# Linear attention and Fourier feed-forward on one core: the second sweep's preparation set on a grid of points, its first pair read from SBUF, weights run through in alternating direction

## The chip, the cores and the metric

The kernel runs on one core of one Trainium2 chip. The metric is the time of one execution in microseconds (us); lower is better. The kernel before was timed three times: 1113.9, 1119.21 and 1117.34 us, median 1117.34.

The engines are named as in the profile: PE (matrix multiplications; PEld is its loading of weights, which overlaps), DVE (vector engine), ACT (scalar engine), POOL (GpSimd), SP (which here issues nearly all DMAs). Each works through its own queue in order; semaphores tie the queues together.

## What is computed

The reference, cut to what matters (8 batches, 8 heads, 576 tokens, head size 64, so 4608 tokens of width 512; hidden width 2048):

```python
kv  = einsum('bhsd,bhse->bhde', k, v)
out = einsum('bhsd,bhde->bhse', q, kv)
x   = (out / rms(out) * g_norm), heads side by side     # [8, 576, 512]
u   = x + real(fft(fft(x, axis=1), axis=2))
un  = (u - mean(u)) / sqrt(var(u) + 1e-6)
result = u + max(un @ w_ch1, 0) @ w_ch2
```

## The kernel before

The 4608 tokens are 9 blocks of 512 (BT), each of 4 tiles of 128 (TPB). The hidden width is 16 slices of 128, called f. Each float32 product is made of three passes (high times high, high times low, low times high), so a 512-wide product over 512 channels is 12 matmuls.

**Stage 1** (until about 362 us in the profile) does attention, Fourier transform and the slices f = 0 to 2 of the feed-forward for every block. A planner (`Plan`) sets its order. It leaves in DRAM: `u_scr` (the tokens u), `part_scr` (the feed-forward part of f = 0 to 2), and `unT_scr` (the normalised tokens, transposed, high and low part; the scaling by 1/sqrt(var) is still missing, it is applied later as `scale`).

**First sweep** (37 steps, L1529 to L1554). One step is one block j and one slice f: `first` (12 matmuls and a relu, split by ACT and DVE into `hh` and `hl`) and then `second` of the step before it (12 matmuls into 4 accumulators). All 9 blocks run f = 3 to 5; block 0 (`LONE`) runs the remaining f = 6 to 15 as well, and thereby finishes. Beside it `sum_w` and `split_w` (one of 20 units in each of the first 20 steps) convert the weights of f = 6 to 15 from their 64-bit input and write them to `w1_scr` and `w2_scr`, in NG = 5 quarters g of two slices. The results of f = 3 to 5 of blocks 1 to 8 go to DRAM as `next_scr` (ACT copies into one of 3 `lp` buffers, L1513, then a DMA, L1514).

**Second sweep** (L1561 to the end). Blocks 1 to 8 form 4 pairs: (8, 7), (6, 5), (4, 3), (2, 1). A loop of 20 rounds (4 pairs times 5 quarters) does in each 7 products `mult` of 6 matmuls each and 8 tile outputs of 6 matmuls each, 90 matmuls in all. The 7 products are Strassen's scheme: two blocks and two slices are combined into sums, so 7 products stand for 8. Every round loads its quarter's weights, `w1c` (1792 KB, `load_w1c`) and `w2c` (1024 KB, `load_w2c`), into one of two buffers. Each pair must be prepared:

- `prep_u`: read 8 tiles of u (`us`), take their variance on DVE (`bn_stats`, L1476), make `scale` of it with ACT's square root and four tiny DVE operations, and write `scale` to DRAM. Tiles whose tokens stand in mirrored order are read by an indirect DMA that POOL issues (L1462).
- `prep_z`: read `unT_scr` back (z and `low`), add the two on POOL (L1608), read `scale` back spread over all partitions (`wide`), multiply on POOL (L1610).
- `prep_t`: three new differences and one in place on POOL (L1618 to L1621).
- `prep_b`: split each of the 7 operands into high (ACT, L1360) and low (DVE, L1361).
- `prep_acc`: read `part_scr` and `next_scr`, add them on POOL (L1637), scale on ACT (L1485), add to `us` on POOL (L1488).

The first pair's preparation stands in the program after the first sweep's end; that of pair p+1 is written behind the rounds of pair p, and the operands are split in the last of them (`turn_over`). Where each instruction lands in its engine's queue is left to the scheduler after 300 us of the plan (`PIN_UNTIL`); only `plan.pin` ties instructions to the order in which they are written.

Of the kernel before, what the change touches and what calls it, by code (L numbers as in the profile page):

```python
# [9 lines left out]
F32 = mybir.dt.float32  # L10
# [9 lines left out]
EPS = 1e-6  # L20
# [273 lines left out]
def kernel(  # L294
# [52 lines left out]
    left = ExitStack()  # L347
    base = left.enter_context(tc.tile_pool(name="base", bufs=1))
    wA = left.enter_context(tc.tile_pool(name="wA", bufs=1))
# [970 lines left out]
    wB1[0].tile([P, PAD_RIGHT // 4], F32, name="pad_right")  # L1320
# [4 lines left out]
    mid = left  # L1325
    work = mid.enter_context(tc.tile_pool(name="work", bufs=1, reuse_waits="tile"))
    extra = mid.enter_context(tc.tile_pool(name="extra", bufs=1, reuse_waits="tile"))
    wq = mid.enter_context(tc.tile_pool(name="wq", bufs=2, reuse_waits="tile"))
    lone_pool = mid.enter_context(tc.tile_pool(name="lone", bufs=1, reuse_waits="tile"))

    LONE = 0
    PAIRS = [(j, j - 1) for j in range(NBLK - 1, 0, -2)]
# [136 lines left out]
    def fetch_block(j, tile_):  # L1469
        mv = tiny.tile([P, TPB, 2], F32, name="bmv")  # L1470
        uts = []
        for i in range(TPB):
            ut = tile_()
            fetch_u(j, i, ut)
            st = tiny.tile([P, 6], F32, name="bst")
            nc.vector.bn_stats(st, ut)  # L1476
# [6 lines left out]
    def add_part(j, i, ut, part, scale):
        t = j * TPB + i
        nc.scalar.activation(  # L1485
            part, part, AF.Identity, scale=scale[:, i : i + 1], bias=p0c[:, t : t + 1]
        )
        nc.gpsimd.tensor_tensor(ut, ut, part, ALU.add)  # L1488

    def lone_in():  # L1490
        lone["u"], lone["scale"] = fetch_block(
            LONE, lambda: lone_pool.tile([P, DM], F32, name="lu", tag="lu", bufs=TPB)
        )
        for i in range(TPB):
            n = LONE * TPB + i
            part = lone_pool.tile([P, DM], F32, name="lp", tag="lp", bufs=3)
            nc.sync.dma_start(part, part_scr[n * P : (n + 1) * P])
            acc = lone["acc"][i]
            nc.gpsimd.tensor_tensor(acc, acc, part, ALU.add)
            add_part(LONE, i, lone["u"][i], acc, lone["scale"])  # L1500

    def second(seg, hpair, f):
        j, fs = seg
        for i in range(TPB):
# [6 lines left out]
            if j != LONE:  # L1511
                part = lone_pool.tile([P, DM], F32, name="lp", tag="lp", bufs=3)
                nc.scalar.copy(part, acc_t[i])  # L1513
                nc.sync.dma_start(next_scr[t * P : (t + 1) * P], part)  # L1514
            elif fs is first_fs:
                part = lone_pool.tile([P, DM], F32, name="la", tag="la", bufs=TPB)
                nc.scalar.copy(part, acc_t[i])
                lone.setdefault("acc", []).append(part)
            elif f < NF - 1:
                part = lone["acc"][i]  # L1520
                nc.vector.tensor_tensor(part, acc_t[i], part, ALU.add)
            else:
                ut = lone["u"][i]
                nc.vector.scalar_tensor_tensor(
# [333 lines left out]
```

## Time and profile before

The profiled execution took 1116.74 us; its span from first to last instruction is 1114.9 us.

| engine | busy us | share of span | instructions |
|---|---|---|---|
| PE | 984.7 | 88% | 5950 |
| PEld | 819.4 | 73% | 5950 |
| DVE | 686.0 | 62% | 1198 |
| ACT | 392.7 | 35% | 747 |
| POOL | 500.1 | 45% | 434 |

The DMAs moved 235.71 MB, 211 GB/s on average; the largest shares are w1c (20 loads of 1792 KB) and w2c (20 loads of 1024 KB). The clock granted to PE was 0.949 of full speed on average. PE is the busiest engine, but its 88% is an average over stages that differ: the stretches in which it waits are what a change to the order of other work can reach.

### The profile page before, as it was taken

What the parts mean: (1) busy time and instruction counts of PE and PEld (TensorE: products, weight loads), DVE (VectorE), ACT (ScalarE), POOL (GpSimd) and SP (SyncE); (2) the same over time, 40 slices, a digit from 0 to 9 for tenths busy, and PEclk for the clock granted to TensorE, in tenths of its full rate; (3) what the DMA queues carried; (4) which work ended last, traced back from release to release, by engine and by line L of the source; (5) the groups of instructions that cost most, each with busy time, mean ns of one, the idle gap of its engine ahead of it and who ended that gap; (6) DMA issues with size and microseconds to landing.
All of it is one profiled execution on the core that took longest, in us unless ns stands there. A gap on an engine that the chain in (4) does not pass through costs nothing.

```text
span 1114.9 us, 16128 instructions
## 1 busy us (share of the span) xinstructions
PE 984.7 (88%) x5950; PEld 819.4 (73%) x5950; DVE 686.0 (62%) x1198; ACT 392.7 (35%) x747; POOL 500.1 (45%) x434
## 2 busy tenths in 40 slices
PE   5999999999999999899950259999869996999998
PEld 4888898888788887788840147777658875888887
DVE  4697877676986899942204236465546754575554
ACT  3557556565442443322310123151114311241110
POOL 2648767856531444430543567664257324700000
PEclk9999999999999999999985579999889998899999
DMA  9899858735568895663786258679756775445422
GB/s 224 224 221 246 265 150 229 216 129 198 194 215 293 302 361 193 259 249 126 255 269 269 48 131 276 190 245 347 190 131 253 290 236 173 174 185 179 155 91 76
DMA packets 130627, 235.71 MB, mean 211 GB/s; under 512 B 57982, under 2 KB 83122, under 8 KB 120052
## 3 DMA queue, kind: packets, MB, share of 16 engines
q1 hardware_dynamic: 126868, 227.07, 62.8%
q0 software_dynamic: 1920, 6.29, 2.2%
q10 hardware_dynamic: 1760, 1.31, 0.4%
q8 instruction: 47, 0.77, 0.3%
q14 instruction: 32, 0.26, 0.1%
HBM read 164.61 MB, written 70.03 MB: 210 GB/s over the span
## 4 chain that ended last, share of the span: by engine, by line
PE 62%; DMA 19%; DVE 7%; POOL 6%; issue 4%; ACT 1%; SPq 0%; POOLq 0%; DVEq 0%; ACTq 0%
PE acc L1685 12%; PE ps_h L1652 9%; DMA up<-next_scr 7%; PE acc L493 6%; PE ps_h L475 6%; PE ps_h L1441 6%; PE acc L1452 6%; PE ps_o L754 4%; PE ps_f L908 4%; DMA us<-u_scr,rowidx 2%; PE ps_k L659 2%; PE ps_f L968 2%; DMA next_scr<-lp 2%; POOL up L1637 2%; DMA z<-unT_scr 2%
## 5 line engine op out<-in xcount | busy, mean ns | idle before, releaser
L1685 PE MATMUL acc<-w2c,hh 128*128 128x512 f32 x640 | 202.7, 399 | 11.1 <-issue 11.1
L488 DVE SCALAR_TENSOR_TENSOR hl<-ps_h,hh 128x512 fp32r<-128x512 f32 x144 | 98.2, 686 | 135.7 <-ACT hh L485 135.0
L485 ACT ACTIVATE hh<-ps_h 128x512 fp32r<-128x512 f32 x144 | 84.9, 594 | 242.2 <-PE ps_h L1441 84.2
L1652 PE MATMUL ps_h<-b,w1c 128*128 128x512 f32 x360 | 97.6, 408 | 62.6 <-ACT b L1360 51.5
L1685 PEld LDWEIGHTS acc<-w2c,hh 128*128 128x128 f32 x640 | 123.7, 194 | 39.2 <-issue 12.6
L1652 PE MATMUL ps_h<-t,w1c 128*128 128x512 f32 x480 | 123.7, 408 | 32.3 <-ACT t L1360 18.9
L1652 PEld LDWEIGHTS ps_h<-t,w1c 128*128 128x128 f32 x480 | 94.1, 198 | 55.8 <-ACT t L1360 19.6
L1695 DVE TENSOR_TENSOR us<-acc,us 128x512 f32<-128x512 f32 (+1 forms) x161 | 106.4, 679 | 38.2 <-PE acc L1685 37.5
L1652 PEld LDWEIGHTS ps_h<-b,w1c 128*128 128x128 f32 x360 | 70.1, 197 | 80.5 <-ACT b L1360 52.0
L1685 PE MATMUL acc<-w2c,hl 128*128 128x512 f32 x320 | 126.6, 396 | 0.0
L1637 POOL TENSOR_TENSOR up<-up,up 128x512 f32<-128x512 f32 x32 | 46.8, 1463 | 62.3 <-DMA up<-next_scr 50.7
L1685 PEld LDWEIGHTS acc<-w2c,hl 128*128 128x128 f32 x320 | 61.6, 192 | 13.3
L1485 ACT ACTIVATE up<-up,p0c,rs_yb 128x512 f32<-128x512 f32 x32 | 25.9, 814 | 127.0 <-POOL up L1637 122.1
L794 POOL TENSOR_TENSOR x<-x,gb 96x512 f32<-96x512 f32 (+1 forms) x42 | 53.6, 1296 | 33.0 <-ACT x L771 21.8
L493 PE MATMUL acc<-w,hh 128*128 128x512 f32 x216 | 67.6, 399 | 0.0
L475 PE MATMUL ps_h<-unTh,w 128*128 128x512 f32 x216 | 67.6, 394 | 0.0
L1476 DVE BATCH_NORM_STATS2 bst<-us 128x6 f32<-128x512 f32 x32 | 21.1, 680 | 66.4 <-DMA us<-u_scr,rowidx 38.0
L1452 PE MATMUL acc<-w,hh 128*128 128x512 f32 x216 | 61.3, 390 | 0.0
L1441 PE MATMUL ps_h<-unTh,w 128*128 128x512 f32 x192 | 59.5, 391 | 1.4 <-DVE wa L1354 1.4
L1669 DVE TENSOR_TENSOR ps_h<-ps_h,s 128x512 f32<-128x512 f32 x60 | 40.1, 694 | 31.3 <-ACT s L1741 22.4
L1608 POOL TENSOR_TENSOR z<-z,low 128x1024 f32<-128x1024 f32 x16 | 39.9, 2493 | 39.0 <-DMA z<-unT_scr 28.5
L1610 POOL TENSOR_TENSOR z<-z,wide 128x1024 f32<-128x1024 f32 x16 | 38.7, 2437 | 38.0 <-DMA wide<-scale_scr 28.8
(178 smaller groups left out, 2072.5 us busy)
## 6 DMA issues: line engine op xcount, KB each, us to landing
w1c<-w_scr SPq DMA_DIRECT2D x20, 1792.0 KB
w2c<-w_scr SPq DMA_DIRECT2D x20, 1024.0 KB
raw<-in_moe_w_ch_dram SPq DMA_DIRECT2D x32, 512.0 KB
unT_scr<-unTh SPq DMA_DIRECT2D x9, 1024.0 KB
unT_scr<-unTl SPq DMA_DIRECT2D x9, 1024.0 KB
part_scr<-part SPq DMA_DIRECT2D x36, 256.0 KB
w_scr<-w1q SPq DMA_DIRECT2D x5, 1792.0 KB
km<-in_k_dram SPq DMA_DIRECT2D x32, 256.0 KB
```

What stands on the lines that cost most here:

```text
L475: nc.tensor.matmul(ps, w[c][:, kc * P : (kc + 1) * P], unT[a][:, kc, :], start=(idx == 0), stop=(idx == 3 * KC - 1),)
L485: nc.scalar.activation(hh, ps, AF.Relu)
L488: nc.vector.scalar_tensor_tensor(hl, ps, 0.0, hh.bitcast(F32), ALU.max, ALU.subtract)
L493: nc.tensor.matmul(acc, hpair[a][:, i * P : (i + 1) * P], w[c], start=(first and n == 0), stop=(last and n == 2),)
L754: nc.tensor.matmul(pss[s].t[:n, at : at + D], fqs[side].t[half, m, :n], kvt.t[half, m], start=True, stop=True,)
L794: nc.gpsimd.tensor_tensor(v_, v_, gb[:n].unsqueeze(1).to_broadcast([n, H, D]), ALU.mult)
L1441: nc.tensor.matmul(ps, w1_of(f, c, kc), unTs[j][a][:, kc, :], start=(idx == 0), stop=(idx == 3 * KC - 1),)
L1452: nc.tensor.matmul(acc, hpair[a][:, i * P : (i + 1) * P], w2_of(f, c), start=(first_ and n == 0), stop=(last_ and n == 2),)
L1637: nc.gpsimd.tensor_tensor(two_[0], two_[0], two_[1], ALU.add)
L1652: nc.tensor.matmul(ps, w[:, A_OF[m], c, kc * P : (kc + 1) * P], b[:, a, kc * BT : (kc + 1) * BT], start=(fresh and idx == 0), stop=(done a ...
L1685: nc.tensor.matmul(ps, hpair[a][:, i * P : (i + 1) * P], w2c[n][:, r, c], start=(idx == 0), stop=(idx == 5),)
L1695: nc.vector.tensor_tensor(ut[:, cols], ps[:, cols], ut[:, cols], ALU.add)
```

## The change

The arithmetic of the result stays; what moves is where and when the second sweep is prepared.

- Pairs are now (2, 1), (8, 7), (6, 5), (4, 3). Blocks 3, 2, 1 are the last of the first sweep, so the transposed tokens of blocks 2 and 1 still lie in SBUF (`unTs`). `z_from` adds them there, without reading `unT_scr` again. `second` adds the f = 3 to 5 result of these two blocks straight from PSUM to `us` (one DVE operation a tile) instead of passing it through `next_scr`.
- From step 28 (`closing`, block 3's first) the first pair's preparation stands in the first sweep, at a step number for each job. For this the buffers move: `base` goes to the right side of SBUF, and the left side is given to the second sweep at step 28.
- From step 28 on everything is pinned (`plan.pin`): each of the five queues keeps the order in which it is written.
- In the rounds, 15 points are counted (after each of the 7 products and 8 outputs, 6 matmuls apart); each job of the next pair's preparation has a point. z is read in halves of 256 KB into 3 `low` buffers. `part_scr` and `next_scr` tiles are no longer added to one another: each is scaled on ACT and added to `us` on POOL (`more_part`), 16 of each a pair instead of 8 ACT operations and 16 POOL ones.
- Odd pairs go through the quarters backwards. A quarter that is still in a buffer isn't loaded again: 14 loads of `w1c` and of `w2c` instead of 20.
- In the first sweep the 20 weight units are spread to one every 1.3 steps, with 5 `wa`, 3 `wp` and 4 `lp` buffers, and `split_w` follows `sum_w` by two steps.

```diff
-    left = ExitStack()
-    base = left.enter_context(tc.tile_pool(name="base", bufs=1))
+    low_ctx = ExitStack()
+    base = low_ctx.enter_context(tc.tile_pool(name="base", bufs=1, side="right"))
...
-    PAIRS = [(j, j - 1) for j in range(NBLK - 1, 0, -2)]
+    PAIRS = [(2, 1)] + [(j, j - 1) for j in range(NBLK - 1, 2, -2)]
...
+    unit_at = {round(n * 1.3): n for n in range(len(units))}
...
+    for j in (7, 8, LONE, None, 6, None, 5, None, 4, None, None, 3, 2, 1):
...
+            if j in PAIRS[0]:
+                nc.vector.scalar_tensor_tensor(
+                    us[j][i], acc_t[i], scale_of[j][:, i : i + 1], us[j][i], ALU.mult, ALU.add
+                )
...
+    def sides(step):
+        if step - LAG in unit_at:
+            split_w(*units[unit_at[step - LAG]])
+        if step in unit_at:
+            units_in(unit_at[step] + 3)
+            sum_w(*units[unit_at[step]])
+        for job in jobs.pop(step, ()):
+            job()
...
+    def low_slot():
+        return lop.tile([P, BT], F32, name="low", tag="low", bufs=3)
...
+    def w1_in(n):
+        g = quarter(n)
+        if w_held.get(("1", g)) == n - 1 or w_held.get(("1", g)) == n - 3:
+            w1c[n] = w1c[w_held["1", g]]
+        else:
+            t = w1c[n] = wcp[g % 2].tile([P, 7, 2, HK], F32R, name="w1c", tag="w1c")
+            nc.sync.dma_start(t.rearrange("p q c n -> p (q c n)").bitcast(F32), w1_scr[g])
+        w_held["1", g] = n
...
+    s0 = closing
+    for s_, j in enumerate(PAIRS[0]):
+        for i in range(TPB):
+            at(s0 + s_, u_in, j, i, lambda: us_slot(0))
+            at(s0 + 2 + s_, u_stats, j, i)
+            at(s0 + 3 + s_ + (i > 1), part_in, j, i, part_scr, low_slot)
+            at(s0 + 4 + s_ + (i > 1), lambda j=j, i=i: add_part(
+                j, i, us[j][i], parts[j, i].pop(0), scale_of[j]
+            ))
+        at(s0 + 2 + s_, u_scale, j)
+        at(s0 + 2 + s_, scale_out, j)
+        at(s0 + 4 + s_, wide_in, j)
+        for k_ in range(2):
+            at(s0 + 2 + 3 * s_ + k_, z_from, 0, s_, k_)
+            at(s0 + 5 + s_, z_scale, 0, s_, k_)
+    at(s0 + 5, w1_in, 0)
+    at(s0 + 6, w2_in, 0)
+    at(s0 + 6, split_b, 1)
+    at(s0 + 6, differ, 0)
+    at(s0 + 7, differ, 1)
+    at(s0 + 7, differ, 2)
+    at(s0 + 7, split_b, 6)
+    at(s0 + 8, differ, 3)
+    for m in (5, 7, 2, 4, 3):
+        at(s0 + 8, split_b, m)
...
+    for n in range(1, total):
+        at(PTS * n - 13 if n > 1 else 0, w1_in, n)
+        at(PTS * n + 1 if n > 1 else 0, w2_in, n)
+    for p in range(1, NP):
+        o = (p - 1) * NG * PTS
+        for n in range(8):
+            s_, k_, c = n // 4, n // 2 % 2, n % 2
+            at(o + 2 + 3 * n, z_in, p, s_, k_, c)
+            at(o + 2 + 3 * n + 7, z_sum, p, s_, k_, c)
+            j, i = PAIRS[p][n // TPB], n % TPB
+            at(o + 18 + n + n // 2, u_in, j, i, lambda p=p: us_slot(p))
+            at(o + 25 + n + n // 2, u_stats, j, i)
+        for s_, j in enumerate(PAIRS[p]):
+            at(o + 31 + 6 * s_, u_scale, j)
+            at(o + 32 + 6 * s_, scale_out, j)
+            at(o + 37 + 6 * s_, wide_in, j)
+            for k_ in range(2):
+                at(o + 43 + 5 * s_ + 2 * k_, z_scale, p, s_, k_)
+        for n in range(4):
+            at(o + 52 + 2 * n, differ, n)
+        for n in range(16):
+            ...
+            at(o + 40 + 3 * n, part_in, j, i, src, up_slot)
+            at(o + 40 + 3 * n + 7, more_part)
```

Three places in the queues show what moved. The first is POOL where the first pair is prepared. Before, behind the first sweep, it issues the reads of u for the second pair (us_6930 to us_6972) ahead of those of the first, and adds `part_scr` and `next_scr` tiles (up2) before it scales z:

```order
L1462 DMA us_6972<-u_scr_87,rowidx_85 128x512
L1637 TENSOR_TENSOR up2_6797<-up2_6797,up2_6799 128x512
L1462 DMA us_6679<-u_scr_87,rowidx_85 128x512
L1462 DMA us_6684<-u_scr_87,rowidx_85 128x512
L1462 DMA us_6689<-u_scr_87,rowidx_85 128x512
L1462 DMA us_6711<-u_scr_87,rowidx_85 128x512
L1462 DMA us_6716<-u_scr_87,rowidx_85 128x512
L1462 DMA us_6721<-u_scr_87,rowidx_85 128x512
L1637 TENSOR_TENSOR up2_6804<-up2_6804,up2_6806 128x512
L1488 TENSOR_TENSOR us_6674<-us_6674,up2_6797 128x512
L1488 TENSOR_TENSOR us_6679<-us_6679,up2_6804 128x512
L1610 TENSOR_TENSOR z11_6741<-z11_6741,wide_6739 128x1024
```

Now, in steps 33 to 36 of the first sweep, the last 12 POOL operations of that preparation are these (L1478 adds a part to u, L1667 makes z from SBUF, L1672 scales it, L1677 and L1682 are the differences; z11 and z21 were made and scaled just ahead):

```order
L1478 TENSOR_TENSOR us_6405<-us_6405,low_6586 128x512
L1478 TENSOR_TENSOR us_6407<-us_6407,low_6588 128x512
L1667 TENSOR_TENSOR z12_6635<-unTh_6468,unTl_6469 128x1024
L1478 TENSOR_TENSOR us_6409<-us_6409,low_6629 128x512
L1478 TENSOR_TENSOR us_6411<-us_6411,low_6631 128x512
L1672 TENSOR_TENSOR z12_6635<-z12_6635,wide_6633 128x1024
L1667 TENSOR_TENSOR z22_6677<-unTh_6468,unTl_6469 128x1024
L1672 TENSOR_TENSOR z22_6677<-z22_6677,wide_6633 128x1024
L1677 TENSOR_TENSOR z1_6685<-z12_6635,z11_6466 128x1024
L1677 TENSOR_TENSOR z2_6720<-z22_6677,z1_6685 128x1024
L1682 TENSOR_TENSOR z12_6635<-z22_6677,z12_6635 128x1024
L1677 TENSOR_TENSOR z4_6755<-z21_6517,z2_6720 128x1024
```

The z operations stand behind the u additions of the same block, and the last one makes z4. The second place is DVE in the rounds. Before, two variances stand together between the outputs (us) of a finishing pair:

```order
L1695 TENSOR_TENSOR us_6706<-acc_7770,us_6706 128x512
L1476 BN_STATS bst_7811<-us_7809 128x6
L1476 BN_STATS bst_7816<-us_7814 128x6
L1695 TENSOR_TENSOR us_6711<-acc_7779,us_6711 128x512
L1477 BN_AGGR bmv_7808<-bst_7811 128x2
L1477 BN_AGGR bmv_7808<-bst_7816 128x2
L1695 TENSOR_TENSOR us_6716<-acc_7788,us_6716 128x512
```

Now each has its point, at least one output apart from the next where the points allow it, and 7 points behind the read of its tile:

```order
L1494 BN_STATS bst_7030<-us_6947 128x6
L1495 BN_AGGR bmv_7029<-bst_7030 128x2
L1819 TENSOR_TENSOR us_6405<-acc_7035,us_6405 128x512
L1494 BN_STATS bst_7043<-us_6958 128x6
L1495 BN_AGGR bmv_7029<-bst_7043 128x2
L1819 TENSOR_TENSOR us_6407<-acc_7046,us_6407 128x512
L1819 TENSOR_TENSOR us_6409<-acc_7057,us_6409 128x512
L1494 BN_STATS bst_7065<-us_6980 128x6
```

The third place is DVE around the first round's products. Before, the last split of the first pair, t4's, stands between the first round's own sums (L1669), and the other six ahead of them:

```order
L1361 TENSOR_TENSOR t3_6783<-z12_6755,t3_6783 128x1024
L1669 TENSOR_TENSOR s1_6874<-ps_h_6867,s1_6865 128x512
L1669 TENSOR_TENSOR ps_h_6876<-ps_h_6876,s1_6874 128x512
L1361 TENSOR_TENSOR t4_6789<-z4_6769,t4_6789 128x1024
L1669 TENSOR_TENSOR ps_h_6867<-ps_h_6886,s1_6874 128x512
```

Now, at the end of the first sweep, five splits (L1362, their names are those of the products' operands) come ahead of the first sweep's last four additions (L1537) and of the first round's own sums (L1794).

```order
L1362 TENSOR_TENSOR t1_6757<-z1_6685,t1_6757 128x1024
L1362 TENSOR_TENSOR t3_6760<-z12_6635,t3_6760 128x1024
L1362 TENSOR_TENSOR b21_6763<-z21_6517,b21_6763 128x1024
L1362 TENSOR_TENSOR t4_6766<-z4_6755,t4_6766 128x1024
L1362 TENSOR_TENSOR b22_6769<-z22_6677,b22_6769 128x1024
L1537 SCALAR_TENSOR_TENSOR us_6405<-acc_6704,rs_yb_6536,us_6405 128x512
L1537 SCALAR_TENSOR_TENSOR us_6407<-acc_6708,rs_yb_6536,us_6407 128x512
L1537 SCALAR_TENSOR_TENSOR us_6409<-acc_6712,rs_yb_6536,us_6409 128x512
L1537 SCALAR_TENSOR_TENSOR us_6411<-acc_6716,rs_yb_6536,us_6411 128x512
L1794 TENSOR_TENSOR s1_6825<-ps_h_6818,s1_6812 128x512
```

Before, all seven splits of the first pair stood behind the first sweep, and none ahead of work of the first sweep.

More of the change, by code (lines that the diff above doesn't have):

```diff
@@ L1483, in add_part @@
[L1483 to L1486, printed above, removed]
-        )
[L1488 to L1500, printed above, removed]
+    def add_part(j, i, ut, part, scale, bias=True):
+        t = j * TPB + i
+        if bias:
+            nc.scalar.activation(
+                part, part, AF.Identity, scale=scale[:, i : i + 1], bias=p0c[:, t : t + 1]
+            )
+        else:
+            nc.scalar.activation(part, part, AF.Copy, scale=scale[:, i : i + 1])
+        nc.gpsimd.tensor_tensor(ut, ut, part, ALU.add)
@@ new lines, with one @@
+    for i in range(TPB):
+        at(closing - 14 + i, lone_u, i)
+        at(closing - 9 + i, u_stats, LONE, i)
+        at(closing - 8 + i, part_in, LONE, i, part_scr, part_slot)
+        at(closing - 5 + i, lone_sum, i)
+        at(closing - 2 + i // 2, lone_add, i)
+    at(closing - 5, u_scale, LONE)
+    units_in(2)
+    load_unT(LONE)
+    LAG = 2
+    slot_now = part_slot
+    def one(step, prev):
+        seg, f = flat[step]
+        j, fs = seg
+        if f == fs[0] and j != LONE:
+            ahead = [s_[0] for s_, _ in flat[step + 1 :] if s_[0] not in loaded]
+            if ahead and step:
+                load_unT(ahead[0])
+        hpair = first(j, f)
+        if prev:
+            second(*prev)
+        return seg, hpair, f
@@ L1561 @@
+    def sides(step):
[6 more added lines that the diff above has]
+            job()
+    prev = None
+    for step in range(closing):
+        prev = one(step, prev)
+        sides(step)
+    prev = one(closing, prev)
+    mid.close()
     end = ExitStack()
@@ new lines, in output @@
+        ps = bank("acc")
+        idx = 0
+        for r in range(2):
+            hpair = hs[n, r, side]
+            for a, c in passes:
+                nc.tensor.matmul(
+                    ps, hpair[a][:, i * P : (i + 1) * P], w2c[n][:, r, c],
+                    start=(idx == 0), stop=(idx == 5),
+                )
+                idx += 1
+        ut = us[j][i]
+        t = j * TPB + i
+        halves = 2 if final and i == TPB - 1 else 1
+        for h in range(halves):
+            cols = slice(h * DM // halves, (h + 1) * DM // halves)
+            nc.vector.tensor_tensor(ut[:, cols], ps[:, cols], ut[:, cols], ALU.add)
+            if g == NG - 1:
+                (nc.scalar if h else nc.sync).dma_start(out[t * P : (t + 1) * P, cols], ut[:, cols])
@@ L1749 @@
         turn_over(7)
-        outputs(n - 1, 0)
+        for i in range(TPB):
+            output(n - 1, 0, i)
+            tick()
         mult(a, 2, n, False, True)
```

359 lines of the change are left out of this document (176 added, 183 removed).

## Prediction

> **What bounds the kernel now.** I began with the page's 40 slices (27.9 us each; digits are tenths busy).
>
> ```profile
> PE   5999999999999999899950259999869996999998
> ...
> POOL 2648767856531444430543567664257324700000
> ```
>
> PE has nines nearly everywhere, so it is the bound, except in slices 21 to 24 (counting from 1) and in later dips (8, 6, 6); POOL is never full. The windows price these places. Columns: start:end, length, busy us of PE, PEld, DVE, ACT and POOL with instruction counts, clock, DMA share, GB/s. First a stretch in which PE never stops, then all from the first sweep on:
>
> ```profile
> 957.48:1094.84 137.36, 137.36 (x607) 113.74 (x607) 81.05 (x117) 33.16 (x51) 12.46 (x8) 1.00 0.42 150
> ```
>
> ```profile
> 362.80:572.20 209.40, 204.10 (x907) 168.15 (x906) 127.72 (x190) 71.54 (x124) 80.31 (x66) 1.00 0.68 247
> 572.20:624.30 52.10, 0.63 (x3) 0.19 (x1) 13.45 (x44) 5.53 (x11) 16.14 (x15) 0.53 0.66 241
> 624.30:671.50 47.20, 22.23 (x68) 16.32 (x69) 18.38 (x16) 11.70 (x15) 31.95 (x16) 0.68 0.47 104
> 671.50:780.00 108.50, 104.67 (x449) 84.10 (x447) 63.46 (x92) 32.78 (x51) 68.33 (x40) 0.99 0.79 263
> 780.00:850.00 70.00, 55.34 (x217) 44.36 (x218) 36.32 (x66) 12.41 (x22) 35.55 (x22) 0.90 0.65 187
> 850.00:895.00 45.00, 45.00 (x200) 37.26 (x199) 33.13 (x43) 16.58 (x24) 18.77 (x10) 1.00 0.69 252
> 895.00:950.40 55.40, 44.29 (x169) 34.85 (x168) 31.02 (x57) 10.22 (x18) 20.72 (x15) 0.88 0.66 213
> 950.40:1111.20 160.80, 160.75 (x703) 132.57 (x701) 92.71 (x136) 35.06 (x54) 19.54 (x12) 0.99 0.40 143
> 1111.20:1114.90 3.70, 0.00 (x0) 0.00 (x0) 0.75 (x2) 0.00 (x0) 0.00 (x0) 0.90 0.39 142
> ```
>
> The single row gives 137.36/607 = 0.2263 us a matmul. So a step of the first sweep (24 matmuls) is worth 5.43 us, a point of the new grid (6) 1.36, a round (90) 20.4, a pair (5 rounds) 102. From 362.8 on there are 907+3+68+449+217+200+169+703 = 2716 matmuls, worth 614.6. With stage 1 (362.8) and the tail (3.7) that makes 981.1, the floor of this work at this rate. The span is 1114.9, so 133.8 are lost: 4.1 in the first sweep (209.4 − 907 × 0.2263), 83.2 in gap and stutter from 572.2 to 671.5 (99.3 − 71 × 0.2263), 46.5 behind them.
>
> The chain of waits (start, length, what) tells what the gap is made of:
>
> ```profile
> 533.33 2.39 DMA next_scr<-lp
> 535.80 3.13 DMA lp<-part_scr
> ...
> 577.32 11.76 DMA w1c<-w_scr
> 589.14 16.04 DMA up<-next_scr
> 607.02 8.89 DMA scale_scr<-rs_yb
> ...
> 647.24 14.15 DMA z<-unT_scr
> ```
>
> One after another: reads in a full queue, the round trip of scale, z of the second block; PE has nothing to do meanwhile. The later losses look like this in the timeline (start, duration, instruction; in brackets the idle time before and what ended it):
>
> ```profile
> 774.55 0.94 POOL L1462 DMA_INDIRECT us<-u_scr,rowidx  x1 [2.28 <-DMA out_dram<-us]
> ...
> 783.92 0.69 DVE L1476 BATCH_NORM_STATS2 bst<-us 128x6 f32<-128x512 f32 x1 [7.62 <-DMA us<-u_scr,rowidx]
> ...
> 785.31 1.19 PE L1685 MATMUL acc<-w2c,hh 128*128 128x512 f32 x2 [5.65 <-issue]
> ```
>
> A u read is issued 9.4 us before the variance that needs it. DVE's queue is in order, the outputs behind the variance wait, and PE stops. From 670 on this is a large wait of DVE's (total us, times, longest); under it the time of such a read from the answer on `us`:
>
> ```profile
> DVE bst L1476 <- DMA us<-u_scr,rowidx: 38.0, 7, 11.6
> ```
>
> ```profile
> DMA to landing us min/median/max: 7.8/7.9/9.3
> ```
>
> **The change, part by part.** Stage 1 is taken as it is: 0.
>
> *First sweep, 4.1 now.* While weights are converted DVE is nearly full:
>
> ```profile
> 368.00:440.00 72.00, 72.00 (x325) 59.59 (x324) 67.73 (x101) 31.22 (x56) 34.89 (x30) 1.00 0.77 280
> ```
>
> 67.73 of 72 is 5.1 of each 5.43 us step, 0.7 of it the step's own relu (page row below), 4.4 a unit. One unit in 1.3 steps makes 4.4/1.3 + 0.7 = 4.1 a step: room. Bounds 0 and the 4.1 of before; I take 1.5, nearer to none.
>
> *Transition, 83.2 now.* Let T be the start of step 28. Nine steps (48.9), the last `second` (2.7) and round 0's 42 matmuls (9.5) let round 1 start at T+61 if nothing waits. What has to be done by then:
>
> ```profile
> L1485 ACT ACTIVATE up<-up,p0c,rs_yb x32: 800/815/818, 604.2 to 968.7; 128x512 f32<-128x512 f32 x32
> L1488 POOL TENSOR_TENSOR us<-us,up x32: 1262/1290/1318, 606.5 to 969.6; 128x512 f32<-128x512 f32 x32
> ```
>
> ```profile
> L1610 POOL TENSOR_TENSOR z<-z,wide x16: 2337/2382/3389, 620.9 to 950.6; 128x1024 f32<-128x1024 f32 x16
> ...
> L1360 ACT ACTIVATE t<-z x16: 1042/1056/1068, 644.4 to 992.5; 128x1024 fp32r<-128x1024 f32 x16
> L1361 DVE TENSOR_TENSOR t<-z,t x16: 1210/1222/2824, 646.7 to 993.7; 128x1024 fp32r<-128x1024 f32 x16
> ```
>
> (min/median/max ns). The parts of blocks 2 and 1 share three `low` buffers with the `next_scr` copies of block 3, whose sums end at about T+21 (3 steps, a `second` and its copies). Four writes and the first read, 2.4 and 3.1 each in the chain above, part of them behind a 2 MB load of `unT_scr`, and ACT's scaling put the first addition on POOL at about T+31. From there POOL has 8 additions at 1.29 and 10 operations on z at 2.38, in one fixed order: 34.1, so z4 is there at T+66. Behind it on DVE are the splits of t4 and b22 (1.06 + 2 × 1.22 with ACT's half), then four additions, four sums and four relus at 0.69 (rows below): 3.5 + 8.3, T+78; the first relu and its output bring T+79. 79 − 61 = 18 lost. What is queued behind the waiting splits is just this: the sums of the last step and of round 0, and PE behind them. Bounds: if parts land 10 us sooner, 8; if one more transfer takes 14 to 16 as in the gap (rows 647.24, 589.14), 34. I take 18. The scale round trip (8.89) and the u reads (16.04 in the full queue) are hidden by the five steps, 27 us, between read and use; without that cover they would cost that again.
>
> *Rounds, 46.5 now.*
>
> ```profile
> L488 DVE SCALAR_TENSOR_TENSOR hl<-ps_h,hh 128x512 fp32r<-128x512 f32 x144 | 98.2, 686 | 135.7 <-ACT hh L485 135.0
> ...
> L1669 DVE TENSOR_TENSOR ps_h<-ps_h,s 128x512 f32<-128x512 f32 x60 | 40.1, 694 | 31.3 <-ACT s L1741 22.4
> ```
>
> u is now read 7 points (9.5 us) ahead of its variance, and landed in 7.8 to 9.3: enough, by 0.2 to 1.7. In a turn round DVE has 4 sums, 4 relus, 8 outputs (additions of the sums' shape) and 7 splits: 2.8 + 2.7 + 5.5 + 8.5 = 19.5 of 20.4 us. POOL now adds parts beside the splits (the last points of `more_part` lie there); a split beside a POOL operation took up to 2.8 instead of 1.2. Two such a turn cost 3.2, 0.9 has room: about 2 in each of three turns. I take 6; bounds 0, and 46 if stalls only change their name. By the medians alone (1222) the turns would lose nothing, and the sum would be 6 less, 1002. The Trainium skill ("SBUF — State Buffer", Who interferes with whom) states that a DVE instruction with two SBUF inputs contends with a GpSimd instruction that reads SBUF, and that the other one blocks; the longest split (2824) and the longest scaling of z (3389) agree with it, so by this page the longest rows would be the ones to use, as done here.
>
> *Additional work of a pair in the rounds.* ACT has 16 scalings instead of 8, at 0.81: 13 of 102 us. POOL has 24 operations on 128x512 at 1.29 (16 parts, 8 sums of z in halves), 8 on 128x1024 at 2.39 and at most 8 u reads at 0.95: 58 of 102. Both lie beside PE's rounds: 0. Should POOL fall behind its points, that is the second rival.
>
> *Removed.* The `next_scr` round trip of blocks 2 and 1 (4 MB) and the second reading of their `unT_scr` (4 MB) were part of the gap's queue and are counted there; the four additions a block that DVE does in place of ACT's copies are in the transition's sum.
>
> *Weights.* Six reloads fewer, 6 × 2.8 = 17 MB. Every round reloads, the stretch 957 to 1095 too (150 GB/s × 137 us = 20.6 MB moved), and PE has no gap there: the reloads were hidden, 0 gained, with the round's 20.4 us as cover. A gain could come only where the queue is full, and there its rate is this:
>
> ```profile
> 594.00:596.00 2.00, 0.00 (x0) 0.00 (x0) 0.00 (x0) 0.00 (x0) 0.00 (x0) 0.50 1.02 427
> ```
>
> 17 MB at 427 GB/s are 41 us of transfer, of which none was waited for outside the gap. These were 256 KB reads of u and parts, so reading z in halves of that size costs 0 by this row. The Trainium skill speaks against the halves ("DMA: Bandwidth & Descriptors", Bandwidth): batch to 1 MiB or more to get 75% of peak. By that page the halves would be slow and the time would go towards that of the third rival; the trace disagrees, 427 GB/s with pieces of 256 KB, many under way at once, and by the row the sum stays.
>
> Sum: 981.1 + 1.5 + 18 + 6 = 1006.6, against a span of 1114.9. 1.84 lie around the span (1116.74 − 1114.9): **1008**. The profiled execution is 0.6 below the median of the runs (1117.34); I leave that out.
>
> **The rivals.**
>
> *The transition is hidden wholly.* For it: PE needs z4 for one of the 7 products only, and has the others to do meanwhile. Against it: 34 us of POOL in one order. Lost 2 instead of 18: 1008 − 16 = 992. Chance 0.13.
>
> *The stall on u stays, in fixed order.* 22 of the 32 u reads are issued by POOL (indirect), now behind sums, scalings and parts that themselves wait for DMAs. One operation on z in front (2.4) makes a read of 7.9 land 0.8 after its point (10.3 − 9.5), one of 9.3 land 2.2 after it; over the 24 tiles of three pairs 19 to 53, in the middle 36 in place of 6, since DVE's outputs and with them PE wait as in the timeline above. For it: POOL idles for DMAs already and waits in order. Against it: 58 of 102 us leave room to run ahead, and points are written so that reads stand apart. 1008 + 30 = 1038. Chance 0.25.
>
> *The halves don't overlap.* A pair reads 40 pieces of 256 KB (16 of z, 8 of u, 16 parts). At the 3.13 of `lp<-part_scr` one after the other they take 125 us of the pair's 102: 23 too long, three times, 1008 + 69 = 1077. Against it the 427 GB/s above. Chance 0.03.
>
> *Slower: SP's fixed order holds the weights back.* SP now issues w1c's load 13 points (17.7 us) ahead of its round, in order behind everything else. The load took 11.8 in the gap: 5.9 of room. Then PE waits at the start of a round for all that SP is late beyond this, in 13 rounds that still load. Before, SP's order was chosen by the scheduler and its waits had these lengths (total, times, longest):
>
> ```profile
> SPq L1646 <- PE acc L1685: 40.8, 7, 20.0
> ```
>
> With SP late by 20.0 each time the price is 13 × (20.0 − 5.9) = 183: 1191. It decides for slower than before from 13 × 8.4 = 109 on (1117), with SP late by 14.3 in each. Against it: this 20.0 is the longest of 7, their mean is 5.8, inside the room. Chance 0.04.
>
> *It doesn't do what it says.* The preparation is written into the first sweep, but its waits could hold that sweep's PE instead of the gap: ACT's scalings of parts stand ahead of the relus of steps 32 to 36, so a late part holds a relu and PE behind it. If the transfers of two blocks' parts each come late by one of the gap's long ones (14.2 and 16.0), and the 8 hidden elsewhere falls away, 1008 + 30 − 8 = 1030. Chance 0.05.
>
> **How the numbers follow.** Forecast: 984.4 (981.1 + 1.5 + 1.8) with 18 between 8 and 34 and 6 between 0 and 46; both near their ends together is rarer, 8 + 2 to 34 + 12 give 995 to 1030, chance 0.50; the rivals 0.13, 0.25, 0.03, 0.04, 0.05. The range reaches down to the hidden transition with nothing lost in the rounds (992 − 4, 988) and up to the stall on u at 47 of its 53 (1008 + 41 = 1049, rounded to 1050): it holds the forecast, most of the first two rivals and the last, 0.85, and leaves out the two large ones and the ends. 0.5% (5.6 us) is about what a measurement of this kernel can tell from no change. Only the slower rival and some of the halves' tail come to 1112 or above: faster 0.95, same 0.01, slower 0.04.
>
> **What would show it.** In the changed kernel's windows from the first sweep's start: 2716 matmuls at 0.2263 again, and the stretch between step 36 and round 1 with about 18 us less than full PE, not 83; in the chain there POOL's z operations and the splits of t4 and b22, where reads stood. In the rounds, few us on the variance's wait for u, and these only in turn rounds; a large sum there is the second rival, many gaps at the starts of rounds that wait for w1c the slower one. DVE under 90% while weights are converted shows the first step. Wrong from the ground would be a clock below 0.95 in the rounds with PE full, or PE's waits in steps 31 to 36 of over 20 us.

## The result and the profile after

The changed kernel took 1036.79 us (median of four, 1031.09 to 1038.9), the kernel before beside it 1118.28; the ratio is 0.9263, with a 95% interval of 0.9209 to 0.9316. It is faster, by 7.4%. The forecast was 1008 in a range of 988 to 1050: the direction is right and the time lies inside, but 29 us above the number. The profiled execution has a span of 1034.4 us and took 1036.17, so the question is where 27.8 us over the summed 1006.6 come from. One execution of the changed kernel, in a repetition reported below, took 1947.94 us; it is left out of all comparisons.

The slices of the page, and windows over the corresponding stages (columns as in the prediction):

```profile
PE   5999999999999999999995679989999999999998
...
POOL 1547777766644113335630853294628553751000
```

```profile
362.80:530.00 167.20, 167.20 (x749) 138.78 (x748) 124.26 (x183) 64.09 (x111) 74.52 (x65) 1.00 0.73 264
530.00:610.00 80.00, 53.13 (x180) 39.55 (x179) 27.54 (x46) 19.88 (x29) 34.38 (x18) 0.79 0.58 140
...
670.00:710.00 40.00, 35.73 (x150) 28.70 (x149) 29.25 (x36) 19.54 (x28) 30.80 (x16) 0.96 0.50 172
...
770.00:810.00 40.00, 36.63 (x154) 29.60 (x153) 23.17 (x29) 16.59 (x24) 28.34 (x15) 0.96 0.55 164
...
890.00:912.00 22.00, 19.12 (x84) 15.19 (x83) 14.20 (x16) 9.95 (x14) 21.25 (x11) 1.00 0.53 201
912.00:1030.70 118.70, 118.70 (x525) 98.03 (x523) 67.17 (x102) 28.35 (x46) 14.13 (x10) 1.00 0.35 122
```

At 0.2263 us a matmul the first sweep loses nothing up to 530. From 530 to 610 the loss is 80 − 180 × 0.2263 = 39.3, where 83.2 were lost before. In the three turn rounds it is 6.1 + 5.2 + 3.0 = 14.2, where 46.5 were lost behind the gap before. Against the terms of the sum:

| stage | forecast, us lost | measured |
|---|---|---|
| first sweep | 1.5 | 0 |
| transition | 18 | 39.3 |
| rounds | 6 | 14.2 |
| sum | 25.5 | 53.5 |

The difference, 28.0, is the whole error. Divided at the end of step 36 (590.69), the transition's loss lies mostly inside the first sweep:

```profile
532.17:590.69 58.52, 41.60 (x145) 30.97 (x143) 14.84 (x34) 12.67 (x20) 21.55 (x13) 0.83 0.66 144
590.69:610.00 19.31, 9.36 (x26) 6.80 (x26) 10.84 (x9) 6.97 (x8) 12.83 (x6) 0.64 0.40 143
```

In steps 31 to 36 it is 58.52 − 145 × 0.2263 = 25.7 us, and behind them 13.4. Not all of it is idle time: PE stood still for 80 − 53.13 = 26.9 us of the 39.3, and the other 12.4 are matmuls that ran at a lower granted clock after each stop, here twelve of them in 5.0 us instead of 2.7 (clock 0.54):

```profile
555.48:560.48 5.00, 5.00 (x12) 3.73 (x13) 0.82 (x3) 0.81 (x1) 1.28 (x1) 0.54 0.88 193
```

In the transition the timelines of SP, ACT, PE and POOL, one row or more from each, show a wait that the forecast didn't have:

```profile
535.45 0.38 SPq L1503 DMA_DIRECT2D scale_scr<-rs_yb  x1
535.92 0.46 SPq L1431 DMA_DIRECT2D unTh<-unT_scr  x1
536.47 0.38 SPq L1431 DMA_DIRECT2D unTl<-unT_scr  x1
536.94 18.23 SPq L1543 DMA_DIRECT2D next_scr<-low  x4
```

```profile
554.25 0.59 ACT L1542 COPY low<-acc 128x512 f32<-128x512 f32 x1 [16.53 <-DMA next_scr<-low]
...
554.84 0.59 ACT L486 ACTIVATE hh<-ps_h 128x512 fp32r<-128x512 f32 x1
```

```profile
555.48 1.22 PE L1453 MATMUL acc<-w,hh 128*128 128x512 f32 x2 [9.55 <-ACT hh L486]
```

```profile
558.94 1.28 POOL L1478 TENSOR_TENSOR us<-us,low 128x512 f32<-128x512 f32 x1 [31.48 <-ACT low L1473]
...
600.32 3.35 POOL L1677 TENSOR_TENSOR z<-z,z 128x1024 f32<-128x1024 f32 x1
```

The write of `scale` (2 KB) is issued first, then 2 MB of `unT_scr`, then block 3's writes to `next_scr`. The copies have three `low` buffers, so ACT's fourth copy waits 16.5 us for the first of the writes to `next_scr` to land, the relu stands behind the copy, and PE behind the relu. What moves meanwhile is almost nothing:

```profile
535.50:545.50 10.00, 10.00 (x46) 8.29 (x45) 3.92 (x10) 2.01 (x4) 0.00 (x0) 1.00 1.06 30
```

That is 30 GB/s in the ten microseconds behind the write of `scale`, which goes out as 512 single floats. (Behind the second write, issued at 556.25, more moved: 85 GB/s from 556.5 to 566.5, not the 27 that the first expectation below gives for both.) The chain of waits ahead of the first turn round begins with the same transfer:

```profile
655.60 12.99 DMA scale_scr<-rs_yb
...
668.61 5.08 DMA wide<-scale_scr
...
679.81 3.44 DMA up<-part_scr
...
683.34 0.81 ACT up L1473
684.15 0.47 ACT s L1876
```

`scale`, `wide` and the parts come one after the other, and ACT's copy of a product's sum stands behind a scaling of parts. So the theory (A): the 4-byte writes of `scale` hold back what is queued behind them. The rival (B): the three `low` buffers, shared by copies and parts, make the wait.

### The profile page after: what moved, and what is told of

The parts are those of the page before. It is cut to its first block, busy times and chain, and to the rows that moved or that the text cites. A ratio compares the mean times of both kernels' runs of the same rounds, so it can differ in the third digit from the quotient of the medians.

```text
span 1034.4 us, 16124 instructions
## 1 busy us (share of the span) xinstructions
PE 978.3 (95%) x5950; PEld 816.5 (79%) x5950; DVE 683.1 (66%) x1206; ACT 402.7 (39%) x763; POOL 495.6 (48%) x438
## 4 chain that ended last, share of the span: by engine, by line
PE 73%; DMA 9%; issue 7%; DVE 6%; POOL 3%; ACT 1%; SPq 0%; DVEq 0%; POOLq 0%; ACTq 0%
PE acc L1809 14%; PE ps_h L1777 13%; PE acc L1453 8%; PE ps_h L1442 8%; PE acc L494 6%; PE ps_h L476 6%; PE ps_o L755 4%; PE ps_f L909 4%; PE ps_k L660 2%; PE ps_f L969 2%; PE ps_s L549 2%; PE ps_q L729 2%; DMA up<-part_scr 1%; DMA low<-unT_scr 1%; DMA scale_scr<-rs_yb 1%
## 5 line engine op out<-in xcount | busy, mean ns | idle before, releaser
L1809 PE MATMUL acc<-w2c,hh 128*128 128x512 f32 x640 | 197.1, 389 | 0.0
L1809 PEld LDWEIGHTS acc<-w2c,hh 128*128 128x128 f32 x640 | 120.1, 188 | 25.1
L1777 PE MATMUL ps_h<-t,w1c 128*128 128x512 f32 x480 | 117.4, 394 | 2.7 <-DVE ps_h L1794 2.7
L1819 DVE TENSOR_TENSOR us<-acc,us 128x512 f32<-128x512 f32 (+1 forms) x161 | 101.8, 678 | 10.2 <-PE acc L1809 9.2
L1478 POOL TENSOR_TENSOR us<-us,up 128x512 f32<-128x512 f32 x48 | 71.4, 1488 | 71.4 <-ACT up L1473 49.5
L1777 PE MATMUL ps_h<-b,w1c 128*128 128x512 f32 x360 | 93.8, 397 | 7.9 <-DMA w1c<-w_scr 6.1
L1453 PE MATMUL acc<-w,hh 128*128 128x512 f32 x216 | 72.3, 426 | 23.9 <-ACT hh L486 23.9
L1453 PEld LDWEIGHTS acc<-w,hh 128*128 128x128 f32 x216 | 44.3, 207 | 35.4 <-ACT hh L486 26.3
L1809 PEld LDWEIGHTS acc<-w2c,hl 128*128 128x128 f32 x320 | 60.1, 188 | 12.4
L1672 POOL TENSOR_TENSOR z<-z,wide 128x1024 f32<-128x1024 f32 x16 | 38.0, 2390 | 62.7 <-DMA wide<-scale_scr 62.6
L494 PE MATMUL acc<-w,hh 128*128 128x512 f32 x216 | 67.6, 399 | 0.0
L1362 POOL TENSOR_TENSOR w1q<-wa,w1q 128x256 fp32r<-128x256 f32 (+1 forms) x15 | 13.8, 926 | 86.6 <-ACT w1q L1361 73.5
L1794 DVE TENSOR_TENSOR ps_h<-ps_h,s 128x512 f32<-128x512 f32 x60 | 39.8, 693 | 13.3 <-PE ps_h L1777 12.7
L1453 PE MATMUL acc<-w,hl 128*128 128x512 f32 x108 | 44.8, 429 | 3.0 <-DVE hl L489 3.0
```

The costliest lines, as they stand in the source:

```text
L494: nc.tensor.matmul(acc, hpair[a][:, i * P : (i + 1) * P], w[c], start=(first and n == 0), stop=(last and n == 2),)
L1453: nc.tensor.matmul(acc, hpair[a][:, i * P : (i + 1) * P], w2_of(f, c), start=(first_ and n == 0), stop=(last_ and n == 2),)
L1777: nc.tensor.matmul(ps, w[:, A_OF[m], c, kc * P : (kc + 1) * P], b[:, a, kc * BT : (kc + 1) * BT], start=(fresh and idx == 0), stop=(done a ...
L1809: nc.tensor.matmul(ps, hpair[a][:, i * P : (i + 1) * P], w2c[n][:, r, c], start=(idx == 0), stop=(idx == 5),)
L1819: nc.vector.tensor_tensor(ut[:, cols], ps[:, cols], ut[:, cols], ALU.add)
```

## The experiments

The times of the kernel before beside these runs were 1108 to 1110 us, so a kernel's own time is compared with 1028.4, which the changed kernel took when run again beside such a time (below).

**16-byte rows.** Each partition writes its four values next to each other, and POOL reads `wide` with that stride.

```diff
-            scale_scr[j : j + 1].rearrange("o (i p) -> p (o i)", p=P), scale_of[j]
+            scale_scr[j : j + 1].rearrange("o (p i) -> p (o i)", p=P), scale_of[j]
...
+        wide = wides[PAIRS[p][s_]].rearrange("p (t i) -> p i t", i=TPB)
...
```

> Theory A (the writes of scale): each writes 2 KB in 512 pieces of 4 bytes and keeps the DMA engines busy for about 9 us at some 27 GB/s (535 to 546 and 557 to 567 in the changed kernel's trace); the unT load, the next_scr writes and the part reads issued just behind it land late by that, ACT waits for them in order, and PE behind ACT. Here the same 2 KB are written as 128 pieces of 16 bytes (the columns of scale lie in another order in DRAM, and the scaling of z reads wide in that order). A: each write takes a quarter, 2 to 4 us; the 38 us lost between 530 and 610 fall by 10 to 16, the time to 1020 to 1027. Theory B (three low buffers shared by the copies and the parts): the copies wait for a buffer all the same; no change beyond 4 us, 1033 to 1040. If the scaling of z with strides is slower on POOL (2.38 now), that adds up to 4 x the difference to the first preparation.

1007.47 us, ratio 0.9082 (0.9057 to 0.9106). Its windows, and the stretch behind the first write of `scale`:

```profile
530.00:610.00 80.00, 62.58 (x243) 48.00 (x242) 36.58 (x61) 23.89 (x36) 46.71 (x26) 0.85 0.60 207
670.00:710.00 40.00, 40.00 (x178) 33.10 (x177) 28.15 (x39) 19.20 (x29) 21.76 (x16) 1.00 0.58 188
770.00:810.00 40.00, 39.97 (x176) 32.75 (x175) 29.31 (x40) 18.13 (x27) 22.55 (x15) 1.00 0.52 168
890.00:912.00 22.00, 22.00 (x98) 18.23 (x98) 13.34 (x22) 7.78 (x13) 9.24 (x7) 1.00 0.40 131
```

```profile
535.50:545.50 10.00, 9.33 (x42) 7.38 (x40) 3.28 (x10) 1.95 (x5) 0.00 (x0) 1.00 0.90 288
```

288 GB/s instead of 30; the transition loses 25.0 instead of 39.3, and the turn rounds nothing at all, which A had not said. The whole gain, 21 us, is above A's 10 to 16, which counted the transition alone. POOL's scaling of z with the stride takes 2.92 instead of 2.40, so the rest is a little more than it had to be.

**Own buffers for block 3's copies**, in two z tiles that are not yet in use.

```diff
+    copies = []
+
+    def copy_slot():
+        if len(copies) % 2 == 0:
+            z_tile(("z1", "z2")[len(copies) // 2])
+        copies.append(z_half(("z1", "z2")[len(copies) // 2], len(copies) % 2))
+        return copies[-1]
...
-    slot_now = low_slot
+    slot_now = copy_slot
```

> Block 3's four copies to next_scr get buffers of their own (in the z1 and z2 tiles, which are not used yet), so ACT's fourth copy doesn't wait for the first write. B: the wait of 16.5 us on ACT and PE's stop of 9.6 us at 545 go and nothing takes their place: 38 us lost fall to 22 or less, 1020 or below. A: the 16.5 us wait goes too, but the reads of the parts still stand behind the slow writes of scale, and ACT waits for them a step later: 1028 to 1036.

1024.26 us, ratio 0.9226 (0.9200 to 0.9253), between the two expectations. These were made from 1036.8; from 1028.4 A's range is 1020 to 1028 and holds it. ACT's waits from 530 to 612 (total us, times, longest) tell more than the time:

```profile
ACT low L1473 <- DMA low<-part_scr: 28.0, 8, 14.5
```

In the changed kernel this wait was 19.7 in all and 5.9 at the longest. The copies' 16.5 us are gone, and the wait stands a step later, on the parts behind the same write: A. B is not the cause, at most 4 us.

**The write of scale issued by ACT.**

```diff
-        nc.sync.dma_start(
+        nc.scalar.dma_start(
             scale_scr[j : j + 1].rearrange("o (i p) -> p (o i)", p=P), scale_of[j]
```

> The writes of scale are issued by ACT instead of SP, all else as in the changed kernel. If the 4-byte pieces hold back only what is queued behind them on SP's queue, the copies' writes and the part reads go on at once: as the 16-byte rows or better, 1018 to 1027. If they occupy the DMA engines themselves, no gain: 1032 to 1040.

1025.6 us in one run, which is within the changed kernel's own spread (1025.0 to 1029.1). The copies' wait fell to 7.3 us (8.0 with 16-byte rows), so in the transition SP's queue is part of the hold-up; the turn rounds still lost about 15 us. From 535.5 to 545.5 it moved 86 GB/s, more than 30 and far from 288. Whether the queue or the engines are held stays open.

**The kernel before with 16-byte rows**, the same edit there.

> The kernel before with the 16-byte rows. There the round trip of scale stands in the gap (8.9 us for the write in the chain of waits) and in each pair's preparation. A: 8 writes are shorter by 6 to 7 us each; what stood on the chain (the first pair's, part of the others') goes: 1095 to 1112. B: no change beyond 6 us, 1111 to 1123.

1069.4 us, ratio 0.9643 (0.9616 to 0.9669): 40 us, more than A expected. The gap and what follows it:

```profile
572.00:671.50 99.50, 38.47 (x148) 29.75 (x147) 44.48 (x76) 22.07 (x33) 69.62 (x38) 0.66 0.64 222
671.50:1063.00 391.50, 382.69 (x1667) 314.83 (x1665) 248.08 (x375) 101.93 (x159) 152.88 (x90) 0.99 0.61 213
```

99.5 − 148 × 0.2263 = 66.0 lost in the gap (83.2 before), and 391.5 − 1667 × 0.2263 = 14.3 in the rounds (46.5). So about two thirds of what the kernel before loses in its rounds hangs on these writes, not on the distance between a u read and its variance. (The trace before is of an execution 7 us longer than the kernel before took beside this run, 1116.74 against 1109.66; if all 7 lay in the rounds, 25 of 39 would hang on them.)

**A spare write** in 4-byte pieces, read by nothing, behind each write in 16-byte rows.

```diff
+        nc.sync.dma_start(
+            spare_scr[j : j + 1].rearrange("o (i p) -> p (o i)", p=P), scale_of[j]
+        )
```

> The 16-byte rows, and behind each write of scale a second one in 4-byte pieces to a place that nothing reads. The real scale is out early, only the DMA engines are kept busy as in the changed kernel. If it is this occupation that cost 20 us, they come back: 1022 to 1032 on this chip. If it was that scale itself arrived late, the spare write costs little: 1007 to 1013.

1025.42 us at the lowest, the other three runs 1044.9 to 1055.3, against 1007.47 without it. The cost is back, at least 18 us; its size rests on the lowest run, as the four spread over 30 us. So it is not the lateness of the real write: a 4-byte write that nobody waits for costs as much, by what stands behind it. The read of `wide` is among this, so whether in the rounds a late `wide` or late parts cost more isn't separated.

**The changed kernel again**, for comparison on one chip with the next three.

> The changed kernel unaltered, for the other runs of this chip to be compared with. The kernel before took 1109.7 on it in the runs above; at the ratio of the result (0.926) 1028, within 5.

1028.44 us, ratio 0.9257 (0.9216 to 0.9298); the result repeats. This median of four has the 1947.94 us in it; the other three are 1025.0 to 1029.05, the middle one 1027.84. The stages of its trace are the base for the runs beside it:

```profile
530.00:610.00 80.00, 53.73 (x196) 39.93 (x194) 30.42 (x51) 20.23 (x30) 36.21 (x19) 0.81 0.59 160
610.00:1022.30 412.30, 403.16 (x1770) 331.67 (x1770) 257.97 (x415) 121.57 (x193) 176.77 (x113) 1.00 0.54 181
```

It lost 35.6 us in the transition and 11.7 from there to the tail, where the first trace lost 39.3 and 15.8. With 16-byte rows these are 25.0 and 1.6: half of the 21 us is the transition's, half the rounds'.

**Weights reloaded in every round**, directions alternating (the same edit for `w2c`).

```diff
-        if w_held.get(("1", g)) == n - 1 or w_held.get(("1", g)) == n - 3:
+        if False:
```

> The changed kernel with every round loading its weights again (20 loads of w1c and w2c instead of 14). All theories of the prediction: the six reloads (17 MB, 41 us at the full queue's rate) are hidden beside 20 us of PE each, 0 to 3 us more than the changed kernel. If they stand in the way of the part and u reads as the writes of scale do, 10 to 20 more, in the turn rounds (the skipped loads are those of the turns).

1084.01 us, ratio 0.9769 (0.9741 to 0.9798): 56 us more, against all theories. PE's longest group of waits from 600 on:

```profile
PE ps_h L1777 <- DMA w1c<-w_scr: 46.5, 9, 11.5
```

The buffer is chosen by the quarter. Where the direction turns, two rounds running need the same quarter, and its load has to wait until the round before has left the only buffer. So this run didn't test the transfers. The next one keeps the edit, and does:

```diff
-        return g if p % 2 == 0 else NG - 1 - g
+        return g
...
-            t = w1c[n] = wcp[g % 2].tile([P, 7, 2, HK], F32R, name="w1c", tag="w1c")
+            t = w1c[n] = wcp[n % 2].tile([P, 7, 2, HK], F32R, name="w1c", tag="w1c")
```

> The changed kernel with all pairs going forwards through the quarters, the buffers in turn by round, and every round loading its weights: as before the change in this one point, with the load of a turn free to start a round ahead. The prediction's theory: reloads are hidden, 0 to 3 us more than the changed kernel (1028 on this chip). If the reload without a second buffer was not what cost 56 us in the run before, but the transfers themselves, 20 to 60 more.

1030.39 us, ratio 0.9284 (0.9248 to 0.9321), whose interval overlaps that of the changed kernel; PE's wait for w1c is 5.9 in all. The 17 MB are hidden, as forecast.

**One weight unit a step**, as before the change.

```diff
-    unit_at = {round(n * 1.3): n for n in range(len(units))}
+    unit_at = {n: n for n in range(len(units))}
```

> The changed kernel with one weight unit in each of the first 20 steps, as before, its buffers and the lag as in the changed kernel. The prediction's theory: DVE needs 5.1 of each 5.43 us step then, and up to 4 us are lost in the first sweep: 1 to 4 more than the changed kernel (1028). If the new buffers and the lag are what helped, no change within 1.

1030.12 us, ratio 0.9310 (0.9263 to 0.9357). The times can't tell it from the changed kernel, the window can:

```profile
440.00:475.00 35.00, 32.37 (x144) 26.12 (x143) 34.86 (x50) 14.60 (x26) 10.89 (x10) 1.00 0.80 312
```

DVE is busy 34.86 of 35, and 35 − 144 × 0.2263 = 2.4 us are lost there, none in the changed kernel. The pace of the units is what helped, by about 2 us.

**16-byte rows and own buffers together**, and then **z ahead of the parts** on POOL (z scaled, made and subtracted before the additions of parts where the order allows it; `wide` read right behind `scale`, and one split a step earlier):

```diff
+        at(s0 + 2 + s_, wide_in, j)
...
+    for k_ in range(2):
+        at(s0 + 3, z_scale, 0, 0, k_)
...
+    for k_ in range(2):
+        at(s0 + 4, z_from, 0, 1, k_)
+        at(s0 + 5, z_scale, 0, 1, k_)
...
+    for n in range(4):
+        at(s0 + 6, differ, n)
```

> 16-byte rows and own buffers for block 3's copies together. With the rows alone 25 us are lost between 530 and 610, and the chain there is POOL's: 8 additions and 10 operations on z from 549 to 588. If POOL's chain bounds it, the copies' buffers bring little more, 0 to 5 us (1002 to 1008); if the shared buffers do, 10 or more (below 998).

> As the one before, with POOL's order in the first sweep changed: wide is read right behind its writing, the first block's z is scaled and the second block's made and scaled before the additions of parts, and the four differences before the last of those. POOL's theory: z4 comes 8 to 15 us sooner and the time falls by that, 990 to 999. If something else holds the transition (ACT's parts ahead of its relus, DVE's splits), no change within 3 of the one before.

1007.67 us (ratio 0.9093, 0.9062 to 0.9124) and 1010.08 us (0.9094, 0.9061 to 0.9126): neither differs from the rows alone (23.7 and 23.9 us lost from 530 to 610, instead of 25.0). The first agrees with POOL's chain as the bound. The second should then have been 8 to 15 us faster, and isn't. ACT's and POOL's rows there, from 525 to 612, say why:

```profile
ACT low L1473 <- DMA low<-part_scr: 24.7, 5, 14.8
...
POOL us L1478 <- ACT low L1473: 6.2, 4, 4.2
```

The reads of the parts now stood behind the wait for `scale` on SP, ACT waited for them ahead of its relus, and the last differences, still behind the additions, ended only some 2 us sooner. So the last run takes the parts away from the first sweep.

**The first pair's parts in rounds 0 to 2.** Additions to `us` can be made in any order before the pair is finished.

```diff
+    for n in range(8):
+        j, i = PAIRS[0][n // TPB], n % TPB
+        at(10 + 2 * n, part_in, j, i, part_scr, up_slot)
+        at(16 + 2 * n, lambda j=j, i=i: add_part(
+            j, i, us[j][i], parts[j, i].pop(0), scale_of[j]
+        ))
```

> As the one before (16-byte rows, own buffers, z first), with the first pair's eight part_scr tiles read, scaled and added in rounds 0 to 2 (points 10 to 30) instead of in the first sweep. If the parts hold the transition (ACT waits 25 us for their reads ahead of its relus, POOL for ACT), PE's stops between 550 and 590 go but for a few us: 25 lost become 3 to 8, 985 to 991 on this chip. If POOL's operations on z or DVE's splits hold it by themselves, at most half goes: 994 to 1003.

996.28 us (995.19 to 998.84), ratio 0.8985 (0.8954 to 0.9016): the fastest of all, 32 us under the changed kernel.

```profile
530.00:610.00 80.00, 71.89 (x304) 58.43 (x303) 43.05 (x71) 25.75 (x39) 46.72 (x28) 0.94 0.68 237
```

80 − 304 × 0.2263 = 11.2 are lost in the transition instead of 25.0. But the next stretch, with the last of the moved additions and the start of the first turn round, loses time in this trace, which is of the longest of the four runs:

```profile
610.00:670.00 60.00, 55.69 (x237) 44.96 (x236) 47.20 (x70) 19.18 (x31) 36.81 (x21) 0.97 0.49 175
```

60 − 237 × 0.2263 = 6.4 are lost here, none with the rows alone; why isn't shown. So by the window the parts were more than half of what was left in the transition, by the time (11 us under the rows alone) a little less, and the time lies in the range of the second expectation, not in that of the parts' theory. PE's two last stops in the transition (4.6 us for ACT's relu, 3.5 for DVE's) stand behind splits that wait for POOL's differences; two of these splits took 5.56 us together, where the prediction's sum had 1.22 for each.

## Why the prediction was right in direction and 29 us short

- **What bounds the kernel** was right. Three places lost PE's time, and the floor held: with the 2729 matmuls recorded here from 362.8 on it is 362.8 + 617.6 + 3.7 = 984.1, against 981.1. (A matmul on the edge of two windows is counted in both; counted in one stretch they are 2714, and 2709 before.)
- **First sweep**, 1.5 forecast, 0 measured. Its reason, DVE full while weights are converted, is shown by the run with one unit a step.
- **Transition**, 18 forecast, 39.3 measured: the step that failed. "Four writes and the first read, 2.4 and 3.1 each" took the writes at their price when nothing stands ahead of them. The first addition came at 558.9. T was 515.9 by the same trace (block 3's sums end at T+21.7, as forecast), so that is T+43 where T+31 was forecast, and T+35 with 16-byte rows. z4 was done at T+88 instead of T+66 (31 and 34.1 make 65): from the first addition on POOL needed 44.7 us where 34.1 were summed, as it waited for later parts and for `wide`. With 16-byte rows it needed 38.7, so some 6 of these 10.6 hang on the second write of `scale`. The prediction had quoted the cause: 8.89 us for `scale_scr<-rs_yb` in the chain. It read the row as a delay of `scale`, hidden by five steps. The steps did hide that; what the transfer did to those queued behind it wasn't asked.
- **The place of that loss.** All 18 were expected behind step 36; there it was 13.4. The 25.7 in steps 31 to 36 are what the last rival (*It doesn't do what it says*, 1030, chance 0.05) described: waits that hold the first sweep's PE. Its own wait, a late part that holds ACT's scaling, the relu behind it and PE, came too:

```profile
564.78 0.81 ACT L1473 ACTIVATE low<-low,p0c,rs_yb 128x512 f32<-128x512 f32 x1 [5.92 <-DMA low<-part_scr]
...
566.13 0.73 PE L1453 MATMUL acc<-w,hh 128*128 128x512 f32 x2 [2.74 <-ACT hh L486]
```

  The longest stop, 9.55, stands behind a copy to `next_scr` instead, which the rival didn't name. PE's idle time in these steps is 16.9 us, under the 20 that were to show the prediction wrong from the ground; with the lower clock behind the stops the loss is above it. So the rival was given too little.
- **Rounds**, 6 forecast, 14.2 measured. PE stood idle there for 10.6 us: 4.5 for sums and outputs on DVE, and the rest for weights, the slower rival's wait in small:

```profile
PE ps_h L1777 <- DMA w1c<-w_scr: 6.1, 2, 3.6
...
685.67 3.45 DVE L1362 TENSOR_TENSOR b<-z,b 128x1024 fp32r<-128x1024 f32 x1 [3.20 <-ACT b L1361]
```

  So the reason given, splits beside POOL's operations, can account for the smaller part only. Such splits did take up to 3.45 us in the turn rounds, 2.38 with 16-byte rows, where these rounds lose nothing and PE has no wait for `w1c`. How much of the 4.5 long splits would cost by themselves isn't shown.
- **The stall on u.** That the 7 points are enough was right; DVE's wait in the changed kernel's rounds (total, times, longest) has gone from 38.0 to

```profile
DVE bst L1494 <- DMA us<-u_scr,rowidx: 1.5, 2, 1.1
```

- The second rival's time (1038) is nearly the measured one, but its mechanism is this wait, so it is refuted. That the time lies in the range is luck in part, as this rival set the upper end; the forecast's own bounds, 995 to 1030, don't hold it. How much of the 46.5 was due to the u reads' place was overrated: 32 of it hang on the writes of `scale` in the kernel before as well.
- **1007.47 us** with 16-byte rows is nearly the forecast by chance: it lost 25.0 and 1.6 where 18 and 6 were forecast.
- **Weights** at 0 and **halves** at 0: right. In the run with 16-byte rows alone all rounds together lost 1.6 us on halves of 256 KB. The third rival didn't occur, and the slower one only with the 6.1 us above. The row quoted for the halves (594 to 596, 427 GB/s) doesn't show them, though: a load of 1792 KB and one of 1024 KB, issued at 584.9 and 585.3, stood ahead of the 256 KB reads. The changed kernel's first halves do: seven were issued from 607.2 to 610.7 behind the 1024 KB load of `w2c` at 606.8, and from 610 to 616 the DMAs moved 342 to 393 GB/s:

```profile
610.00:612.00 2.00, 2.00 (x11) 1.65 (x10) 2.00 (x4) 0.00 (x0) 0.00 (x0) 1.00 0.95 342
...
614.00:616.00 2.00, 2.00 (x10) 1.66 (x10) 1.33 (x3) 1.28 (x3) 2.00 (x2) 1.00 1.06 393
```

Of the change's 82 us, then: with the writes of `scale` out of the way in both kernels it is worth 1069.4 − 1007.5 = 62. The other 20 or so are cost of those writes that the new order happened to avoid.

## What to carry to other kernels

A small transfer is priced twice: by when its data is needed, and by what is queued behind it. Look in the windows for stretches where the DMAs read busy and move a tenth of their rate, and see what was issued just ahead. Work that is moved into a stage in which PE is full brings its waits along: ask which instruction of that stage will stand behind it in each queue. When a wait is taken away by another buffer, look whether the same transfer is waited for one instruction later (16.5 us became 14.5 here) before crediting the edit. A buffer chosen by content instead of by turn loses its prefetch as soon as the content repeats.

## What the hardware showed unexpectedly

A write of 2 KB in 512 pieces of 4 bytes took 8.9 to 13.0 us in the chains; as 128 pieces of 16 bytes it was landed 1.4 us after its issue where SP waited for it (issued 535.34, the read of it at 536.78, in the run with z ahead). Behind the 4-byte write 2 MB and three 256 KB writes were queued, and 30 GB/s moved; in the gap of the kernel before, where little else was queued, the DMA share beside it was small:

```profile
607.00:616.00 9.00, 0.00 (x0) 0.00 (x0) 3.99 (x14) 0.94 (x4) 2.03 (x2) 0.50 0.14 29
```

0.14 here, beside a write of 8.9 us, and 1.06 in the changed kernel with other transfers behind the write. So by this measure the write alone doesn't keep the engines busy; what holds the transfers behind it, the queue or something that the queues share, isn't shown. The skipping read of `wide` with a stride of 16 bytes cost POOL 2.92 instead of 2.40 us a tile.
